# Five added matmuls on zeros at the start of a planned attention and feed-forward kernel, and another table of planner rules

## The chip, the cores and the metric

The kernel runs on one core of a Trainium2 chip. The metric is the time of one execution on the device in microseconds (us). Four compute engines and the DMA queues work side by side and meet only at semaphores: TensorE (PE, matmuls; PEld in the profile is its weight load), VectorE (DVE), ScalarE (ACT) and GpSimd (POOL). SyncE (SP) issues most of the transfers. The profile also has the clock that TensorE was granted, as a share of its full clock.

## The reference

```python
mod = (_silu(c) @ w_mod).reshape(c.shape[0], 6, 1, -1)
sa, ca, ga, sb, cb, gb = (mod[:, i] for i in range(6))         # six rows of 512
h = _layernorm(x) * (1 + ca) + sa
x = x + ga * _A_ref(h, A_wqkv, A_wo)                           # attention, 32 heads of 16
h = _layernorm(x) * (1 + cb) + sb
x = x + gb * ((_gelu(h @ w_gate) * (h @ w_up)) @ w_down)       # 512 -> 1792 -> 512
```

x has 2048 tokens of 512 numbers in bf16. Attention is full: every one of 32 heads has 2048 x 2048 scores, softmax(q k / 4), and then a product with v.

## The kernel before

**Tiling.** Queries are worked on in sets of columns (SETS: seven of 256, two of 128; the first two go together as 512 for the first four groups of heads). For one set and one group of four heads (a "unit"), keys come in tiles of 128. A *slot* is one bank of PSUM, 128 keys by 512 columns of scores. There are 2048 slots, and their order is fixed when the program is written. Scores go to ps_sc, which is two halves of three banks. A *chunk* of two or three slots fills one half (`qk`, recorded at L361 like every matmul), and then one ACT instruction exponentiates it into the tile E (L374). PE multiplies E with the values (`pv_mms`, into ps_pv or the last bank of ps_sc).

**Two engines for the exponential.** ACT does most slots. For some groups of four slots, called *quads*, DVE does it by writing the scaled score as the bits of a bf16 number (uint16, L386, out of ps_sc into kq, dreg, mreg or onorm) and by making three shifted copies of the four slots (128x2048 uint16, L386). PE adds the four versions up with correspondingly scaled values (tile vs). One slot of a quad goes into a chunk beside two slots for ACT.

**Planner.** The kernel is written by a planner that runs when the program is built (`stream`). It keeps a model of each engine's free time, and at each step it records the next instruction in each engine's queue: a chunk of scores, a round of values, a *side* step (projections, feed-forward of finished sets, on ps_mi), a filler matmul, or a DVE task (`step`, `background`). Engines then run their queues in that order, and only semaphores hold them. The planner puts in filler matmuls (`filler`) when the matmul columns that it has logged in the last 3413 ns are under FILL = 3700. The added matmuls are logged too.

**Rules.** The planner's choices follow a tuple of 14 numbers, `self.tune`. The table TUNE has 33 of them, and `rules` takes the row of the current stage, that is of the slot position divided by STEP = 64. The rules, numbered from 0: 0 how far ACT must be ahead before other work goes in front of scores; 1 the credit of side work under which a quad may be opened late; 2 the backlog of DVE tasks at which no quad is opened; 3 how far ahead DVE tasks may go before a quad's slot; 4 and 5 how late DVE may be (after the present, after ACT) when it takes a slot; 6 and 7 when a quad's shifted copies become urgent, by the rounds left in its unit; 8 and 9 how near and how far a quad's slots may lie; 10 and 11 the credit that lets a side step go in front; 12 the rate of that credit in per cent; 13 how far ahead DVE's background tasks are placed.

**The start.** `prologue` loads the first tokens, warms PE up on a tile of zeros (`warm`, 17 matmuls of 128x512 into ps_mi), computes the modulation columns, layer norms, transposes and projects the first 512 tokens for four head groups. At its end ACT and DVE evict queries and keys (qT, kT). Then `stream` takes over; after chunk 0 it calls `prologue_rest` (keys of the second 256 tokens, then the masks of `split_q` on DVE, which clear odd or even heads in the queries), and after chunk 2 `prologue_v`. From `stream` on, `mm` splits a whole matmul into four of 32 output columns (`self.split`).

## Time and profile before

| | us |
|---|---|
| median of three runs (lowest, highest) | 813.16 (811.11, 813.68) |
| the profiled execution | 813.47 |
| its span, first to last instruction | 811.7 |
| busy: ACT, PE, DVE, POOL | 777.2, 751.3, 749.9, 4.9 |
| first exponential of scores, end of the last one | 13.2, 783.8 |
| mean granted TensorE clock | 0.992 |

A line of a group reads: line of the program, engine, operation, tile written, tiles read, shapes and count, then busy time and mean duration of one, then the idle time of the engine just before and what ended it. A line of the timeline has start and duration in us first. A group that merges several instructions has the time from the first start to the last end. A line of the view by stretches has start and end, length, busy time of each engine with its count of instructions, granted clock, share of the DMA engines, and GB/s.

### The profile page before, as it was taken

To read this page: it belongs to the slowest core of one execution; us is meant where nothing else is said; L and a number is where in the kernel's file an instruction comes from. 1 tells how busy PE (TensorE), PEld (TensorE's weight loads), DVE (VectorE), ACT (ScalarE), POOL (GpSimd) and SP (SyncE) were. 2 spreads that over 40 slices of the span, in tenths; PEclk is the share of its full clock that TensorE was granted. 3 is DMA by queue.
4 is the path that set the end of the run, shared out by engine and by line. 5 is a ranking of instruction groups with operands and counts; after the bars stand their busy time and mean duration, and the time that the engine had idled before them with its cause. 6 is when DMAs were issued, how large, how long until landed. Compare 5 with 4: busy or idle time off the path is not lost.

```text
span 811.7 us, 37453 instructions
## 1 busy us (share of the span) xinstructions
PE 751.3 (93%) x17217; PEld 367.2 (45%) x17217; DVE 749.9 (92%) x1512; ACT 777.2 (96%) x746; POOL 4.9 (1%) x13
## 2 busy tenths in 40 slices
PE   7989899998989998998999999999898999998998
PEld 3333334343444454444534444345443543355666
DVE  6776899999999999999999999999999999999963
ACT  5899999999999999999999999999999999999962
POOL 2000000000000000000000000000000000000000
PEclk8799999999999999999999999999999999999999
DMA  9100000012562044104420442025333532300000
GB/s 301 58 2 17 15 10 11 11 28 60 151 206 55 17 139 130 52 16 126 131 69 17 125 122 66 23 61 153 88 75 100 167 96 63 94 10 12 18 12 15
DMA packets 96404, 59.23 MB, mean 73 GB/s; under 512 B 17141, under 2 KB 93814, under 8 KB 96246
## 3 DMA queue, kind: packets, MB, share of 16 engines
q1 hardware_dynamic: 95716, 56.30, 24.7%
q8 instruction: 135, 2.21, 1.1%
q10 hardware_dynamic: 530, 0.53, 0.2%
q14 instruction: 23, 0.19, 0.1%
HBM read 50.04 MB, written 4.18 MB: 67 GB/s over the span
## 4 chain that ended last, share of the span: by engine, by line
ACT 72%; PE 14%; DVE 11%; DMA 2%; issue 1%; SPq 0%; DVEq 0%
ACT E L374 70%; PE ps_sc L361 6%; PE ps_mi L361 5%; PE ps_pv L361 3%; ACT wreg L374 2%; DVE dreg L386 2%; DVE mreg L386 2%; DVE wreg L395 1%; DVE wreg L378 1%; DVE kq L386 1%; DMA mreg<-in_B_w_up_dram 1%; DVE wreg L391 1%; DMA mreg<-in_B_w_gate_dram 1%; DVE wreg L386 0%; DMA xs<-in_A_x_dram 0%
## 5 line engine op out<-in xcount | busy, mean ns | idle before, releaser
L374 ACT ACTIVATE E<-ps_sc 128x1024 bf16<-128x1024 f32 (+2 forms) x700 | 751.6, 1306 | 20.5 <-PE ps_sc L361 20.2
L361 PE MATMUL ps_sc<-qT,kT 32*128 32x256 bf16 (+3 forms) x2048 | 200.0, 274 | 20.9 <-ACT E L374 17.5
L361 PE MATMUL ps_sc<-qo,kT 32*128 32x256 bf16 (+2 forms) x2048 | 197.7, 274 | 17.1 <-ACT E L374 14.7
L361 PE MATMUL ps_pv<-E,vaug 128*17 128x256 bf16 (+2 forms) x3168 | 152.8, 274 | 0.7 <-DVE vaug L395 0.3
L386 DVE TENSOR_SCALAR dreg<-ps_sc 128x512 uint16<-128x512 f32 x208 | 140.3, 683 | 6.4 <-PE ps_sc L361 5.5
L361 PE MATMUL ps_mi<-wreg,mreg 128*32 128x256 bf16 x2816 | 112.0, 275 | 6.5 <-DVE wreg L391 2.2
L361 PEld LDWEIGHTS ps_sc<-qT,kT 32*128 32x128 bf16 (+1 forms) x2048 | 60.4, 92 | 110.4 <-ACT E L374 93.0
L361 PEld LDWEIGHTS ps_sc<-qo,kT 32*128 32x128 bf16 x2048 | 60.2, 92 | 108.5 <-ACT E L374 94.7
L361 PEld LDWEIGHTS ps_pv<-E,vaug 128*17 128x17 bf16 x3168 | 60.2, 89 | 58.0 <-issue 38.7
L361 PEld LDWEIGHTS ps_mi<-wreg,mreg 128*32 128x32 bf16 x2816 | 64.9, 96 | 39.6 <-issue 22.6
L386 DVE TENSOR_SCALAR kq<-ps_sc 128x512 uint16<-128x512 f32 x108 | 72.8, 682 | 5.1 <-PE ps_sc L361 5.0
L386 DVE TENSOR_SCALAR mreg<-ps_sc 128x512 uint16<-128x512 f32 x100 | 67.2, 683 | 2.4 <-PE ps_sc L361 2.1
L361 PE MATMUL ps_pv<-mreg,vs 128*17 128x256 bf16 (+2 forms) x1552 | 67.0, 267 | 2.5 <-issue 1.4
L386 DVE TENSOR_SCALAR mreg<-dreg 128x2048 uint16<-128x2048 uint16 x93 | 62.2, 678 | 0.0
L361 PEld LDWEIGHTS ps_pv<-mreg,vs 128*17 128x17 bf16 x1552 | 33.7, 91 | 14.9 <-issue 5.4
L361 PE MATMUL ps_mi<-hreg,wreg 128*32 128x512 bf16 (+1 forms) x496 | 37.8, 381 | 0.7 <-DVE qT L386 0.6
L395 DVE CAST wreg<-ps_mi 128x512 bf16<-128x512 f32 x49 | 33.4, 681 | 1.0 <-PE ps_mi L361 0.6
L378 DVE TENSOR_TENSOR wreg<-wreg 128x1024 bf16<-128x1024 bf16 (+1 forms) x56 | 34.2, 611 | 0.0
L391 DVE SCALAR_TENSOR_TENSOR wreg<-wreg,ps_mi 128x512 bf16<-128x512 bf16 x49 | 33.2, 678 | 0.9 <-PE ps_mi L361 0.7
L386 DVE TENSOR_SCALAR mreg<-mreg 128x2048 uint16<-128x2048 uint16 x49 | 32.7, 681 | 0.0
L395 DVE COPY osb<-ps_pv 128x256 f32<-128x256 f32 (+2 forms) x63 | 25.9, 411 | 4.9 <-PE ps_pv L361 4.6
L374 ACT ACTIVATE wreg<-wreg 128x1024 bf16<-128x1024 bf16 (+1 forms) x28 | 30.2, 1080 | 0.0
(203 smaller groups left out, 777.6 us busy)
## 6 DMA issues: line engine op xcount, KB each, us to landing
mreg<-in_B_w_up_dram SPq DMA_DIRECT2D x46, 256.0 KB, 3.1
mreg<-in_B_w_gate_dram SPq DMA_DIRECT2D x42, 256.0 KB, 3.2
rb<-scr_rec SPq DMA_DIRECT2D x120, 32.0 KB, 1.9
dreg<-wd_scaled SPq DMA_DIRECT2D x15, 256.0 KB, 3.9
mreg<-wd_scaled SPq DMA_DIRECT2D x10, 256.0 KB, 4.3
ereg<-wd_scaled SPq DMA_DIRECT2D x10, 256.0 KB, 3.8
mreg<-in_w_mod_dram SPq DMA_DIRECT2D x1, 2048.0 KB, 12.4
out_dram<-xs SPq DMA_DIRECT2D x15, 128.0 KB, 1.8
```

The source lines that it names most:

```text
L361: return self.rec("pe", lambda e: e.matmul(out, lhsT, rhs, start=start, stop=stop, tile_position=tp), [lhsT, rhs], [out], cost=(n, int(rhs ...
L374: return self.rec("act", lambda e: e.activation(out, in_, func, scale=scale, **kw), rd, wr, cost=self.cost("act", out, [in_], "act"))
L378: return self.rec(eng, lambda e: e.tensor_tensor(out, a, b, op), [a, b], [out], cost=self.cost(eng, out, [a, b], "tt"))
L386: return self.rec(eng, lambda e: e.tensor_scalar(out, a, s1, s2, **kw), rd, [out], cost=self.cost(eng, out, [a], "ts") + 60 * (len(rd) - 1 ...
L391: return self.rec("dve", lambda e: e.scalar_tensor_tensor(out, a, s, b, op0=op0, op1=op1), rd, [out], cost=self.cost("dve", out, [a, b], " ...
L395: return self.rec(eng, lambda e: e.tensor_copy(out, in_), [in_], [out], cost=self.cost(eng, out, [in_], "ts"))
```

## The change

Two calls are added: one matmul on the tile of zeros behind the last projection of the prologue, and four behind the key projection in `prologue_rest`. Each writes ps_mi, which nobody reads in that state. The one in the prologue is a single 128x128 by 128x512 instruction; the four others are split into four instructions each. And each of the 33 rows of TUNE gets other numbers. No function is changed otherwise. Rows 0 to 10 and 28 to 32 of the old and of the new table, and the two calls:

```diff
 TUNE = (
-    (1000, 4097, 6, 120, 700, 150, 2, 9, 96, 30, 2, 1536, 100, 150),
-    (600, 3500, 6, 120, 700, 150, 2, 3, 96, 30, 2, 1536, 100, 150),
-    (600, 3500, 6, 120, 700, 150, 2, 3, 96, 27, 3, 1536, 100, 0),
-    (600, 3500, 6, 120, 700, 150, 2, 3, 64, 27, 3, 3500, 100, 400),
-    (600, 3500, 5, 120, 700, 150, 2, 3, 96, 30, 2, 3500, 125, 150),
-    (1000, 2500, 5, 120, 700, 450, 2, 3, 96, 30, 2, 3500, 125, 100),
-    (600, 3500, 6, 120, 700, 150, 2, 9, 96, 30, 2, 1536, 100, 150),
-    (600, 3500, 6, 120, 500, 150, 2, 9, 96, 30, 2, 1536, 100, 400),
-    (600, 3500, 6, 120, 700, 150, 4, 9, 96, 30, 2, 1536, 100, 250),
-    (600, 3500, 6, 120, 700, 150, 2, 9, 96, 30, 2, 1536, 110, 150),
-    (600, 3500, 7, 120, 500, 450, 2, 9, 96, 30, 2, 1536, 110, 150),
...
-    (600, 4097, 6, 120, 500, 150, 2, 16, 128, 24, 2, 1536, 125, 400),
-    (600, 4097, 6, 120, 500, 150, 2, 9, 48, 30, 2, 1536, 125, 400),
-    (600, 3500, 6, 120, 500, 0, 2, 16, 96, 34, 2, 1536, 100, 400),
-    (600, 2500, 6, 120, 1100, 150, 2, 9, 96, 30, 0, 1536, 80, 150),
-    (600, 2500, 6, 120, 1100, 150, 2, 9, 96, 30, 0, 1536, 80, 150),
+    (800, 3500, 6, 120, 700, 0, 0, 9, 48, 30, 3, 800, 100, 150),
+    (600, 3500, 6, 60, 700, 450, 2, 16, 96, 30, 2, 1536, 100, 250),
+    (600, 3000, 6, 60, 700, 450, 2, 16, 64, 30, 2, 1536, 100, 400),
+    (600, 3500, 6, 0, 1100, 150, 2, 9, 96, 30, 2, 3500, 110, 400),
+    (600, 3500, 6, 0, 1100, 150, 2, 9, 96, 30, 2, 800, 110, 400),
+    (600, 3500, 6, 0, 1100, 150, 1, 16, 96, 30, 3, 3500, 100, 400),
+    (600, 3500, 5, 120, 500, 450, 2, 3, 96, 34, 2, 2500, 100, 400),
+    (600, 3500, 5, 120, 500, 450, 2, 3, 96, 34, 2, 2500, 100, 400),
+    (1000, 3500, 5, 120, 500, 450, 2, 3, 96, 30, 2, 2500, 125, 400),
+    (1000, 3500, 5, 120, 900, 450, 2, 3, 96, 30, 2, 3500, 125, 400),
+    (600, 4097, 5, 120, 900, 450, 2, 3, 96, 24, 2, 1536, 90, 400),
...
+    (600, 3500, 5, 0, 700, 150, 2, 9, 128, 38, 2, 1536, 80, 150),
+    (450, 3500, 3, 120, 700, 150, 2, 9, 96, 30, 2, 1536, 100, 0),
+    (300, 3500, 6, 0, 700, 150, 2, 6, 128, 24, 2, 1536, 110, 150),
+    (800, 3500, 6, 120, 900, 0, 2, 16, 96, 30, 2, 1536, 100, 150),
+    (800, 3500, 6, 120, 900, 0, 2, 16, 96, 30, 2, 1536, 100, 150),
 )
@@
             for n, dc in enumerate((3, 0, 1, 2) if h == 0 else (2, 0, 3, 1)):
                 for out, col in ((qb[h], 0), (kb, 512))[:2 - h]:
                     self.mm(out, self.wqkv[:, dc, col:col + P], self.hT[:, dc, hs], start=(n == 0), stop=(n == NDC - 1))
+        self.warm_up(1)
         for h in range(2):
             self.act(self.qT[:, 0, 256 * h:256 * h + 256], qb[h], ACT.Copy, scale=Q_SCALE)
         self.copy(dve, self.kT[:, 0, 0:256], kb)
@@
         for dc in range(NDC):
             self.mm(self.pv[:, 256:512], self.wqkv[:, dc, 512:512 + P], self.hT[:, dc, 256:512], start=(dc == 0), stop=(dc == NDC - 1))
+        self.warm_up(4)
         self.copy("dve", self.kT[:, 0, 256:512], self.pv[:, 256:512])
```

## The prediction

> **What bounds the kernel now.** I read the page's slices first, then busy time by stretch, the groups of ScalarE (ACT) and VectorE (DVE), and last the timeline of the first 29 us.

> ```profile
> ACT  5899999999999999999999999999999999999962
> PEclk8799999999999999999999999999999999999999
> 28.80:85.00 56.20, 51.49 (x949) 20.01 (x945) 41.62 (x110) 55.97 (x52) 0.56 (x1) 1.00 0.04 9
> 110.00:745.00 635.00, 592.13 (x13986) 285.24 (x13986) 619.10 (x1174) 634.25 (x603) 0.00 (x0) 1.00 0.29 79
> 783.80:811.70 27.90, 23.36 (x348) 19.60 (x336) 11.87 (x34) 7.05 (x14) 0.00 (x0) 1.00 0.04 11
> ```

> The columns of the last three lines are the stretch, its length, then busy time of PE, PEld, DVE, ACT and POOL, the granted clock, and DMA. From 28.8 to 745 us ACT is never idle to speak of (55.97 of 56.20, 634.25 of 635.00). So the time there is what ACT has to do, and only the hand-over of score slots to DVE makes it less. The last 27.9 us, after the final exponential, are a serial tail. What is left is the start, where PEclk shows an 8 and a 7. The same view cut at the clock's edges:

> ```profile
> 8.13:11.54 3.41, 2.76 (x41) 2.14 (x41) 3.06 (x13) 2.29 (x4) 0.00 (x0) 1.00 1.14 312
> 11.54:14.95 3.41, 1.66 (x29) 0.86 (x28) 1.76 (x6) 2.22 (x3) 0.00 (x0) 1.00 1.10 339
> 14.95:18.37 3.42, 3.26 (x71) 1.75 (x70) 2.04 (x6) 2.49 (x3) 0.00 (x0) 0.50 1.08 357
> 21.78:25.19 3.41, 3.41 (x24) 1.10 (x20) 1.49 (x7) 2.21 (x3) 0.00 (x0) 0.50 0.44 155
> 25.19:28.60 3.41, 3.41 (x36) 0.95 (x33) 2.64 (x14) 2.77 (x3) 0.00 (x0) 0.50 0.02 5
> 28.60:32.02 3.42, 3.23 (x46) 1.37 (x43) 2.92 (x9) 3.21 (x3) 0.00 (x0) 1.00 0.00 0
> ```

> PE was busy for only 1.66 of the 3.41 us before 14.95, and there the clock halves, for 13.65 us. During this time PE is full (3.41 of 3.41), and ACT waits for it. These are ACT's exponentials of that stretch, each with the idle time before it:

> ```profile
> 13.17 1.45 ACT L374 ACTIVATE E<-ps_sc 128x1536 bf16<-128x1536 f32 x1 [0.58 <-PE ps_sc L361]
> 15.46 2.37 ACT L374 ACTIVATE E<-ps_sc 128x1024 bf16<-128x1024 f32 x2 [0.84 <-PE ps_sc L361]
> 18.25 1.02 ACT L374 ACTIVATE E<-ps_sc 128x1024 bf16<-128x1024 f32 x1 [0.42 <-PE ps_sc L361]
> 19.67 2.36 ACT L374 ACTIVATE E<-ps_sc 128x1536 bf16<-128x1536 f32 x2 [0.40 <-PE ps_sc L361]
> 23.23 3.71 ACT L374 ACTIVATE E<-ps_sc 128x1536 bf16<-128x1536 f32 x3 [1.20 <-PE ps_sc L361]
> 27.33 1.02 ACT L374 ACTIVATE E<-ps_sc 128x1024 bf16<-128x1024 f32 x1 [0.39 <-PE ps_sc L361]
> 28.81 1.45 ACT L374 ACTIVATE E<-ps_sc 128x1536 bf16<-128x1536 f32 x1 [0.46 <-PE ps_sc L361]
> ```

> The six waits after the first exponential add up to 0.84 + 0.42 + 0.40 + 1.20 + 0.39 + 0.46 = 3.71 us. ACT runs without a gap afterwards, so what is won here moves everything behind it forward.

> **The change, part by part.** *The five matmuls.* They stand in two holes of PE:

> ```profile
> 11.57 0.60 PE L361 MATMUL ps_sc<-hreg,wreg 128*128 128x256 bf16 x4
> 12.73 0.39 PE L361 MATMUL ps_sc<-qT,kT 16*128 16x512 bf16 x3 [0.56 <-ACT qT L374]
> 13.06 0.62 PE L361 MATMUL ps_pv<-hreg,wreg 128*32 128x256 bf16 x16
> 14.45 0.35 DVE L386 TENSOR_SCALAR qT<-qT,rm 128x512 bf16<-128x512 bf16 x1
> 14.86 0.98 PE L361 MATMUL ps_sc<-qT,kT 16*128 16x512 bf16 x5 [1.19 <-DVE qT L386]
> 20.63 1.47 PE L361 MATMUL ps_mi<-xs,ident 128*32 128x512 bf16 x12
> 28.69 0.40 PE L361 MATMUL ps_mi<-xs,ident 128*32 128x512 bf16 x4
> 7.87 0.38 PE L361 MATMUL ps_mi<-dreg 128*128 128x512 bf16 x1
> ```

> The one of the prologue is a whole 128x512 matmul, 0.38 us to its end, in a hole of 0.56 us: nothing. The four of prologue_rest are split into four instructions each, 16 in all, with as many weight loads. One set takes 0.40 us at full clock; three at half clock took 1.47 us, 0.43 us apart after a first 0.60, so about 0.21 us apart at full clock. Four sets: 3 x 0.21 + 0.40 = 1.04 us, in a hole of 1.19 us. What hides them is DVE, which masks the queries until 14.80 us; the scores behind them on PE need that. Without this cover they would cost their 1.04 us. The evictions wait for earlier matmuls, not for these. The bank that they write, ps_mi, was last read by ACT before 11.54:

> ```profile
> 10.53 1.01 ACT L374 ACTIVATE hreg<-ps_mi,modA 128x256 bf16<-128x256 bf16 x2
> ```

> They add 0.38 + 1.04 us to 1.66, so about 3.1 of 3.41 us busy, more than the 2.76 of the window before, after which the clock stayed whole. I take it that the clock then stays at 1.00.

> Worth: PE's scores come at full speed. Of the first wait (0.84 us) DVE's mask sets most; the scores end 0.2 us sooner (0.39 instead of about 0.6). The other five waits, 2.87 us, stand in a stretch in which PE is the full engine and its work halves; I take them as gone. Gain 0.2 + 2.87 = 3.1 us. Bounds: 3.7 us (all of it) and -0.5 us (the clock halves while they run: four sets at 0.43 are 1.7 us in a hole of 1.19). I take 3.1 because DVE, next in line, is busy for only 1.49 and 2.64 us of the two later windows. Late next is DVE's chain of layer norms, which itself waits for PE there.

> [...]

> *The table.* It changes the order of the work, not its amount, except for the number of quads (four score slots that DVE computes with shifted copies instead of ACT).

> ```profile
> L374 ACT ACTIVATE E<-ps_sc 128x1024 bf16<-128x1024 f32 x448 | 449.5, 1164 | 2.7 <-PE ps_sc L361 2.4
> L374 ACT ACTIVATE E<-ps_sc 128x1536 bf16<-128x1536 f32 x244 | 363.6, 1591 | 4.5 <-PE ps_sc L361 4.5
> L386 DVE TENSOR_SCALAR dreg<-ps_sc 128x512 uint16<-128x512 f32 x208 | 140.3, 683 | 6.4 <-PE ps_sc L361 5.5
> L386 DVE TENSOR_SCALAR kq<-ps_sc 128x512 uint16<-128x512 f32 x108 | 72.8, 682 | 5.1 <-PE ps_sc L361 5.0
> L386 DVE TENSOR_SCALAR mreg<-ps_sc 128x512 uint16<-128x512 f32 x100 | 67.2, 683 | 2.4 <-PE ps_sc L361 2.1
> L386 DVE TENSOR_SCALAR mreg<-dreg 128x2048 uint16<-128x2048 uint16 x93 | 62.2, 678 | 0.0
> ```

> A chunk of three slots keeps ACT for 363.6/244 = 1.490 us, one of two for 449.5/448 = 1.003. A quad takes a slot from each of four chunks: 4 x 0.487 = 1.95 us less on ACT, for 4 x 0.683 + 3 x 0.68 = 4.77 us more on DVE. How many quads the new table gives, no view of this kernel shows. Bounds: DVE idles 56.20 - 41.62 = 14.6 us between 28.8 and 85, room for three more at most, a gain of 5.9 us; three fewer cost as much. I take none, since new rows loosen some rules and tighten others (below). The tail's order may shift by about 1 us either way: the table's last rows touch it, but its 27.9 us are a chain.

> Sum for the profiled execution (813.47 us, its span 811.7 and 1.8 around it): 813.5 - 3.1 = 810.4. It lies 0.3 above the median of the three runs, 813.16; against that median I predict **810.1 us**.

> **The rivals.** *More quads early (806.2).* Rows 1 and 2 raise rule 7 from 3 to 16, which puts the shifted copies ahead of DVE's other tasks and so frees their buffers sooner. For it:

> ```profile
> 56.98 0.69 DVE L386 TENSOR_SCALAR kq<-ps_sc 128x512 uint16<-128x512 f32 x1 [1.14 <-PE ps_sc L361]
> 60.39 0.63 DVE L386 TENSOR_SCALAR sq<-kq 128x2048 uint16<-128x2048 uint16 x1
> 64.57 0.68 DVE L386 TENSOR_SCALAR onorm<-kq 128x2048 uint16<-128x2048 uint16 x1
> 72.35 0.69 DVE L395 CAST vaug<-ps_mi 128x512 bf16<-128x512 f32 x1 [1.71 <-PE ps_mi L361]
> ```

> A quad's last slot is done at 57.7, its last copy only at 65.2. Against it: behind 70 us DVE waits for value projections, which no rule of these rows brings sooner. Two more quads give 810.1 - 3.9 = 806.2.

> *The clock is lost anyway (813.2 to 813.7).* The matmuls do not hold it, because what counts is not PE's busy time: from 21.8 to 25.2 us PE was full and the clock stayed at 0.50, or because a later window falls short. Against: the whole-array zeros are denser work than the tiles of those windows. Time: as before, or up to 0.5 us more. [...]

> *Fewer quads in the middle (816), slower.* Rule 2, the DVE backlog at which no quad is opened, goes from 6, 6, 6, 6, 7 to 5 in rows 6 to 10, and from 6, 6 to 5, 3 in rows 28 and 29. A row holds for 64 of 2048 slots, (783.8 - 13.2)/32 = 24 us; seven rows are 168 us. In the long stretch there are 95 quads:

> ```profile
> L386 DVE TENSOR_SCALAR dreg<-ps_sc 128x512 uint16<-128x512 f32 x192 | 129.5, 683 | 5.7 <-PE ps_sc L361 5.0
> L386 DVE TENSOR_SCALAR kq<-ps_sc 128x512 uint16<-128x512 f32 x96 | 64.6, 682 | 1.4 <-PE ps_sc L361 1.3
> L386 DVE TENSOR_SCALAR mreg<-ps_sc 128x512 uint16<-128x512 f32 x92 | 61.9, 683 | 1.9 <-PE ps_sc L361 1.6
> ```

> (192 + 96 + 92)/4 = 95 in 635 us, so 25 in those rows. ACT has no slack to hide a lost one. It decides from three lost of 25: 3 x 1.95 = 5.9 us against a gain of 3.1 is 2.7 us slower than before, 810.1 + 5.9 = 816.0. Against it: rows 6 to 9 also let DVE run 450 instead of 150 ns behind ACT, which admits more, and a quad refused for backlog can often be opened a chunk later.

> **How the numbers follow.** A measurement of this kernel tells about 0.3% (2.4 us) from no change. Chances: clock held and quads about as many 0.50 (own range 807.5 to 812); more quads 0.13; clock lost 0.15; fewer quads 0.22. Below 810.7 lie the second and four fifths of the first: 0.53. Above 815.6 lie the last and a little of the clock case joined with a lost quad: 0.25. Within: 0.22. The range runs from 805.5 (between two and three quads more) to 816.5 (three fewer and a little).

> **What would show it.** The granted clock at 1.00 from 14.95 to 28.6 us, ACT's waits for scores before 29 us near 0.6 instead of 3.7, the scores after the mask not later than 14.9 us: the first part is right. The count of DVE's 128x512 uint16 writes from ps_sc in the three groups above, now 208 + 108 + 100 = 416, over four gives the quads: 104 means that my zero is right, 101 or fewer the slower rival, 106 the faster. A clock of 0.50 after the added matmuls, or ACT waiting for scores between 29 and 745 us, would make the prediction wrong.

## The result, and the profile after

| | us |
|---|---|
| median of the changed kernel, 22 runs (lowest, highest) | 811.02 (808.65, 816.78) |
| median of the kernel before on the same chip, 22 runs | 815.00 (811.11, 820.90) |
| ratio, with its 95% interval | 0.996 (0.9941 to 0.998) |
| the profiled execution, its span | 808.65, 806.9 (before 813.47, 811.7) |

The change makes the kernel 0.4% faster (0.2 to 0.6%). The profiled executions differ by 4.8 us. The slices of ACT and of the clock of the changed kernel:

```profile
ACT  6999999999999999999999999999999999999972
PEclk9999999999999999999999999999999999999999
```

The clock no longer dips: its mean is 1.000, where it was 0.992. Busy time by stretch of 3.41 us, from the one with the second hole on (columns as before: stretch, length, PE, PEld, DVE, ACT, POOL, clock, DMA):

```profile
12.95:16.37 3.42, 3.10 (x103) 1.75 (x98) 2.65 (x8) 2.75 (x3) 0.00 (x0) 1.00 1.10 331
16.37:19.78 3.41, 2.68 (x31) 0.84 (x29) 3.13 (x13) 3.41 (x4) 0.00 (x0) 1.00 1.05 394
19.78:23.19 3.41, 2.65 (x40) 1.14 (x38) 2.84 (x12) 3.41 (x4) 0.00 (x0) 1.00 1.02 381
```

ACT, which was busy for 2.2 to 3.0 us of such a stretch, has the 0.67 us wait in the first of these three and fills the other two. ACT's timeline of the first 30 us shows one wait behind the first chunk where there were six:

```profile
12.95 1.45 ACT L374 ACTIVATE E<-ps_sc 128x1536 bf16<-128x1536 f32 x1 [0.58 <-PE ps_sc L361]
15.07 15.93 ACT L374 ACTIVATE E<-ps_sc 128x1024 bf16<-128x1024 f32 x14 [0.67 <-PE ps_sc L361]
```

In the timeline of PE and DVE there, the four added sets (16 instructions) lie under DVE's mask:

```profile
12.84 0.62 PE L361 MATMUL ps_pv<-hreg,wreg 128*32 128x256 bf16 x16
13.29 1.04 PE L361 MATMUL ps_mi<-dreg 128*32 128x512 bf16 x16
14.23 0.35 DVE L386 TENSOR_SCALAR qT<-qT,rm 128x512 bf16<-128x512 bf16 x1
14.64 0.60 PE L361 MATMUL ps_sc<-qT,kT 16*128 16x512 bf16 x5 [0.32 <-DVE qT L386]
```

They take the 1.04 us of the sum, and the scores start when the mask ends, with 0.32 us of PE to spare. (The record of the single matmul in the first hole is missing from this trace; its weight load at 11.68 us is there.)

What is left of the 4.8 us is seen in ACT's waits for scores: total, times, longest. The kernel before, in the stretches 14 to 31, 31 to 700 and 700 to 784 us (the first includes the 0.58 us ahead of the first chunk):

```profile
ACT E L374 <- PE ps_sc L361: 4.3, 7, 1.2
ACT E L374 <- PE ps_sc L361: 0.2, 1, 0.2
ACT E L374 <- PE ps_sc L361: 2.3, 4, 1.3
```

The changed kernel, in the same stretches:

```profile
ACT E L374 <- PE ps_sc L361: 1.2, 2, 0.7
ACT E L374 <- PE ps_sc L361: 1.2, 4, 0.5
ACT E L374 <- PE ps_sc L361: 0.7, 2, 0.5
```

4.3 to 1.2 at the start is 3.1 us less (3.71 - 0.67 = 3.04 in the finer rows); 1.0 more in the middle; 1.6 less at the end. The rest of the 4.8 is a first chunk 0.2 us earlier, 0.8 less ACT work between the first and the last chunk (764.1 to 763.3 us without the waits), and a tail shorter by 0.3 us. The number of quads is the same, (208 + 108 + 100)/4 = 104; these are the changed kernel's groups:

```profile
L386 DVE TENSOR_SCALAR dreg<-ps_sc 128x512 uint16<-128x512 f32 x208 | 140.0, 684 | 7.1 <-PE ps_sc L361 6.0
L386 DVE TENSOR_SCALAR kq<-ps_sc 128x512 uint16<-128x512 f32 x108 | 73.3, 684 | 3.7 <-PE ps_sc L361 3.2
L386 DVE TENSOR_SCALAR mreg<-ps_sc 128x512 uint16<-128x512 f32 x100 | 67.1, 682 | 1.0 <-PE ps_sc L361 0.7
```

### The profile page after: what moved, and what is told of

It reads as the page before. It is cut to its first block, busy times and chain, and to the rows that moved or that the text cites. A ratio compares the mean times of both kernels' runs of the same rounds, so it can differ in the third digit from the quotient of the medians.

```text
span 806.9 us, 37455 instructions
## 1 busy us (share of the span) xinstructions
PE 748.4 (93%) x17214; PEld 366.9 (45%) x17218; DVE 749.4 (93%) x1512; ACT 776.5 (96%) x746; POOL 4.6 (1%) x13
## 3 DMA queue, kind: packets, MB, share of 16 engines
q8 instruction: 135, 2.21, 1.1%
## 4 chain that ended last, share of the span: by engine, by line
ACT 80%; PE 11%; DVE 6%; DMA 2%; issue 1%; SPq 0%; DVEq 0%
ACT E L374 77%; PE ps_sc L361 5%; PE ps_mi L361 4%; PE ps_pv L361 2%; ACT wreg L374 2%; DVE dreg L386 1%; DVE mreg L386 1%; DVE wreg L395 1%; DMA scr_rec<-rden 1%; DMA xs<-in_A_x_dram 0%; DMA dreg<-in_B_w_down_dram 0%; DMA rb<-scr_rec 0%; DMA mreg<-in_B_w_up_dram 0%; DVE dreg L378 0%; DVE st L414 0%
## 5 line engine op out<-in xcount | busy, mean ns | idle before, releaser
L374 ACT ACTIVATE E<-ps_sc 128x1024 bf16<-128x1024 f32 (+2 forms) x700 | 751.1, 1312 | 16.6 <-PE ps_sc L361 16.3
L361 PE MATMUL ps_sc<-qT,kT 32*128 32x256 bf16 (+3 forms) x2048 | 197.0, 273 | 20.8 <-ACT E L374 18.6
L361 PE MATMUL ps_sc<-qo,kT 32*128 32x256 bf16 (+2 forms) x2048 | 194.6, 273 | 18.5 <-ACT E L374 15.9
L361 PE MATMUL ps_pv<-E,vaug 128*17 128x256 bf16 (+2 forms) x3172 | 152.5, 272 | 1.7 <-DVE osb L395 0.8
L386 DVE TENSOR_SCALAR dreg<-ps_sc 128x512 uint16<-128x512 f32 x208 | 140.0, 684 | 7.1 <-PE ps_sc L361 6.0
L361 PE MATMUL ps_mi<-wreg,mreg 128*32 128x256 bf16 x2816 | 114.9, 275 | 3.9 <-DVE wreg L395 2.2
L361 PEld LDWEIGHTS ps_sc<-qo,kT 32*128 32x128 bf16 x2048 | 59.8, 92 | 111.2 <-ACT E L374 101.0
L361 PEld LDWEIGHTS ps_sc<-qT,kT 32*128 32x128 bf16 (+1 forms) x2048 | 59.7, 92 | 107.4 <-ACT E L374 94.9
L361 PEld LDWEIGHTS ps_pv<-E,vaug 128*17 128x17 bf16 x3172 | 60.3, 89 | 58.8 <-issue 39.8
L361 PEld LDWEIGHTS ps_mi<-wreg,mreg 128*32 128x32 bf16 x2816 | 64.0, 96 | 39.6 <-issue 23.8
L386 DVE TENSOR_SCALAR kq<-ps_sc 128x512 uint16<-128x512 f32 x108 | 73.3, 684 | 3.7 <-PE ps_sc L361 3.2
L361 PE MATMUL ps_pv<-mreg,vs 128*17 128x256 bf16 (+2 forms) x1528 | 68.8, 268 | 0.1
L386 DVE TENSOR_SCALAR mreg<-ps_sc 128x512 uint16<-128x512 f32 x100 | 67.1, 682 | 1.0 <-PE ps_sc L361 0.7
L386 DVE TENSOR_SCALAR mreg<-dreg 128x2048 uint16<-128x2048 uint16 x93 | 62.6, 680 | 0.0
L361 PEld LDWEIGHTS ps_pv<-mreg,vs 128*17 128x17 bf16 x1528 | 33.3, 90 | 11.8 <-issue 5.1
L361 PE MATMUL ps_mi<-hreg,wreg 128*32 128x512 bf16 (+1 forms) x496 | 37.2, 376 | 0.1
L395 DVE CAST wreg<-ps_mi 128x512 bf16<-128x512 f32 x49 | 33.4, 682 | 1.4 <-PE ps_mi L361 1.2
L386 DVE TENSOR_SCALAR mreg<-mreg 128x2048 uint16<-128x2048 uint16 x49 | 33.2, 680 | 0.0
L374 ACT ACTIVATE wreg<-wreg 128x1024 bf16<-128x1024 bf16 (+1 forms) x28 | 30.4, 1085 | 0.2 <-DVE wreg L378 0.2
L395 DVE COPY osb<-ps_pv 128x256 f32<-128x256 f32 (+2 forms) x63 | 25.9, 411 | 3.2 <-PE ps_pv L361 3.1
```

The lines of the kernel that those rows point to most:

```text
L361: return self.rec("pe", lambda e: e.matmul(out, lhsT, rhs, start=start, stop=stop, tile_position=tp), [lhsT, rhs], [out], cost=(n, int(rhs ...
L374: return self.rec("act", lambda e: e.activation(out, in_, func, scale=scale, **kw), rd, wr, cost=self.cost("act", out, [in_], "act"))
L386: return self.rec(eng, lambda e: e.tensor_scalar(out, a, s1, s2, **kw), rd, [out], cost=self.cost(eng, out, [a], "ts") + 60 * (len(rd) - 1 ...
L395: return self.rec(eng, lambda e: e.tensor_copy(out, in_), [in_], [out], cost=self.cost(eng, out, [in_], "ts"))
```

## The experiments

All ratios are against the kernel before, run on the same chip in the same job. Runs of one kernel differ by several us, for reasons shown in part below, so a profile's waits and the medians are read together. The two profiles above come from quick runs: 808.65 us is the fastest of the 22 runs of the changed kernel, and 813.47 is under the median of the kernel before.

| run | median us (runs) | before | ratio (95%) |
|---|---|---|---|
| five matmuls alone | 812.79 (10) | 816.14 | 0.9949 (0.9930 to 0.9967) |
| table alone | 812.00 (7) | 816.14 | 0.9938 (0.9909 to 0.9967) |
| five thin matmuls | 815.12 (12) | 816.14 | 0.9987 (0.9968 to 1.0006) |
| the change | 810.70 (6) | 816.14 | 0.9929 (0.9906 to 0.9953) |
| last rows new, in the old order | 813.61 (12) | 816.34 | 0.9975 (0.9952 to 0.9997) |
| last rows old, in the new order | 812.82 (12) | 816.34 | 0.9952 (0.9930 to 0.9973) |
| one matmul | 816.68 (10) | 816.34 | 1.0001 (0.9977 to 1.0025) |
| nine matmuls | 814.24 (10) | 816.34 | 0.9976 (0.9956 to 0.9996) |
| the change, holes filled | 811.95 (12) | 813.59 | 0.9975 (0.9957 to 0.9993) |
| the change, third time | 809.52 (12) | 813.59 | 0.9946 (0.9923 to 0.9969) |
| old order, five matmuls, holes filled | 815.50 (12) | 813.59 | 1.0016 (0.9997 to 1.0035) |
| five matmuls alone, again | 812.04 (12) | 813.59 | 0.9983 (0.9961 to 1.0005) |

### Which half of the change gains: matmuls alone, table alone, both

The matmuls are put into the old order behind the planner's back, so that every queue but PE's stays as it was:

```diff
+    def unplanned(self, f):
+        kept = dict(self.free), self.pe_issue, self.pe_end, self.pe_mode, list(self.tile_free), len(self.log)
+        f()
+        self.free, self.pe_issue, self.pe_end, self.pe_mode, self.tile_free, n = kept
+        del self.log[n:]
...
+        self.unplanned(lambda: self.warm_up(1))
...
+        self.unplanned(lambda: self.warm_up(4))
```

> The order of the kernel before, instruction for instruction, with the five matmuls put in and nothing else (the planner does not see them). My theory, that the matmuls hold the clock: granted clock 1.00 throughout, ACT's waits for scores before 29 us fall from 3.7 to about 0.7, time 3.0 to 3.3 us (0.4%) below the kernel before. The rival, that the new order makes the gain: the clock may hold, but less than 1 us is gained, since the old order was written without them.

The other way round, the changed kernel's planner counts the matmuls and they are not issued:

```diff
+    def ghost_up(self, n):
+        for _ in range(n):
+            for j in range(4) if self.split else (None,):
+                self.model(_Op("pe", "pe", 0, None), self.free["pe"], (512, P, None if j is None else (0, 32 * j)))
...
-        self.warm_up(1)
+        self.ghost_up(1)
...
-        self.warm_up(4)
+        self.ghost_up(4)
```

> The order of the changed kernel, instruction for instruction, without the five matmuls (the planner still counts them, so that nothing else moves). My theory: the clock halves near 15 us for some 10 to 14 us, ACT waits 3 us or more for scores there, and the time is 1 to 2 us below the kernel before (what the shorter waits behind 745 us are worth). The rival, that the new order makes the gain: 4 us or more below the kernel before, as the changed kernel.

> The changed kernel itself, on the same chip as the other three, for comparison: 4 to 5 us below the kernel before in the profile; granted clock 1.00 throughout.

Each half gains, and they overlap. ACT's waits in the same three stretches, matmuls alone:

```profile
ACT E L374 <- PE ps_sc L361: 1.3, 2, 0.7
ACT E L374 <- PE ps_sc L361: 0.2, 1, 0.2
ACT E L374 <- PE ps_sc L361: 3.0, 5, 1.3
```

and table alone:

```profile
ACT E L374 <- PE ps_sc L361: 2.9, 5, 0.9
ACT E L374 <- PE ps_sc L361: 2.8, 8, 0.6
ACT E L374 <- PE ps_sc L361: 1.1, 2, 0.8
```

The matmuls do what the theory says, in the start alone: 3.0 us off the waits, 3.35 off the median. The new order takes nothing there that depends on them; behind 700 us it has about two us less of waits than the run with the matmuls alone (3.0 against 0.7, and 0.3 and 1.3 in the two later traces of the change). Without the matmuls its clock halves too, at 15.33 us, but only for 6.8 us instead of 13.65, so that there the matmuls are worth 2.9 - 1.2 = 1.7 us of waits. On this chip the medians are 816.14 before, 812.79 with the matmuls, 810.70 with the table as well; that is 3.35 and then 2.1 us. In the later job the two steps were 1.55 and 2.5 us, and there the matmuls alone are not told from no change (0.9961 to 1.0005). So the size of each step is known to a us or two, no better. My expectation for the table alone, 1 to 2 us, was too low: the medians differ by 4.1 us, the interval of the ratio is 2.7 to 7.4 us. The clock was lost there for a shorter time than I had reckoned. The profiles do not account for the rest. Over all three stretches the table alone waits 6.8 us, as much as the kernel before; the matmuls alone 4.5 us (a trace of the quickest of its ten runs), and the three traces of the change 3.1, 4.7 and 5.5 us. What the new order saves behind 700 us it loses in part between 31 and 700 us (1.2, 3.1 and 2.9 us of waits against 0.2). That the table is worth about 2 us rests on the medians, which agree in direction in both jobs.

### What holds the clock: busy time, or how much of the array works

Five matmuls of the same length at the same places, each on a sixteenth of the array:

```diff
+    def thin_up(self, n, m):
+        for _ in range(n):
+            self.mm(self.mi[0:32, :], self.warm[0:32, 0:32], self.warm[0:32, :], tp=(0, 0))
...
+        self.unplanned(lambda: self.thin_up(1, 1))
...
+        self.unplanned(lambda: self.thin_up(4, 1))
```

> The order of the kernel before, with five matmuls of 512 columns put in at the two places, but each on one corner of 32 rows by 32 columns of the array (a sixteenth), so that PE is busy at the same places. If the clock goes by the share of time in which PE is busy, it holds at 1.00 and the time is as in the run with whole matmuls (3 us below before). If it goes by how much of the array works, which I take for likelier, the clock halves near 15 us as before, and the time is within 0.5 us of the kernel before.

Busy time of the run with thin matmuls, in the window before the clock falls and in the next:

```profile
12.33:15.74 3.41, 2.94 (x57) 1.23 (x60) 1.96 (x6) 2.16 (x3) 0.00 (x0) 1.00 1.10 336
15.74:19.15 3.41, 3.16 (x65) 1.38 (x53) 2.51 (x11) 3.03 (x4) 0.00 (x0) 0.50 1.07 379
```

PE is busy for 2.94 of 3.41 us and the clock halves; in the changed kernel it held after windows with 2.65 and 2.68. So busy time does not sort these windows. (The four in the second hole are one instruction each here, so they also have fewer weight loads; the count that follows does not rest on this run alone.)

The windows are read from the clock itself. In the kernel before it was 1.00 from 4.71 to 14.95 us, 0.50 from there to 28.60 us and 1.00 to the end of the span; the spells of 10.24 and 13.65 us are three and four times 3.41. It was 0.50 for 6.83 us at the start of the run with thin matmuls and of that with the table alone, and for 3.41 us in the second trace of the changed kernel (635.61 to 639.02 us): two and one times. All the spells at half clock in the fourteen traces, up to the last exponential of scores, were one, two or four times 3.41 us long.

I counted every matmul of a window as its columns times the share of 128 x 128, in steps of 32, that its shape fills (a whole 128x512 matmul is 512, a set of four on 32 output columns also 512, scores of three row groups 384). At full clock one whole 128x512 followed the other every 0.216 us (from 805.79 us of the kernel before), so 3.41 us have room for about 8090 such columns. In the same traces, up to the same point, the full clock fell after eighteen windows, which had 2168 to 3076 columns by this count, and was kept after all others, over 3100 windows; the lowest of these had 2943. What these traces show is that overlap, from 2943 to 3076, and not a line within it. The few matmuls in f32 are counted here by their columns, once or twice. They last longer than that: the two instructions of one product on 128 columns, from 787.41 us of the kernel before, took 0.28 us, as long as five times 128 columns at 0.216 us per 512. Counted four times, one of the eighteen (at 759.65 us in the run with one matmul) would have 3524. The share of the array sorts these windows better than the columns alone: counted by the used quarters of the output columns alone, with all rows taken as used, the clock fell after windows with up to 7316 and was kept from 3321 up. Before the change the window from 11.54 us had 2701; with the added 5 x 512 that sum is over 5000, and the clock stayed at 1.00.

The other dose, one matmul alone, tests the count from below:

```diff
+        self.unplanned(lambda: self.warm_up(1))
```

> The order of the kernel before with only the first added matmul, the whole one in the hole of 0.56 us. Counted as columns times the share of the array that works, the window before the clock halves held 2701, and no window under about 3000 kept the clock; 512 more make 3200, just over. My theory, that this sum must stay over about 3000 in every window of 3.41 us wherever the grid of windows lies: one matmul helps in some positions of the grid and not in others, and more often than not the clock still halves near 15 us; gain 0 to 2 us. Rival, that any work in the hole is enough: clock 1.00 before 29 us, gain 3 us.

The ACT timeline of that run begins

```profile
14.98 3.28 ACT L374 ACTIVATE E<-ps_sc 128x1024 bf16<-128x1024 f32 x3 [0.67 <-PE ps_sc L361]
18.59 2.37 ACT L374 ACTIVATE E<-ps_sc 128x1536 bf16<-128x1536 f32 x2 [0.33 <-PE ps_sc L361]
22.15 2.37 ACT L374 ACTIVATE E<-ps_sc 128x1536 bf16<-128x1536 f32 x2 [1.20 <-PE ps_sc L361]
```

and its clock halved at 15.55 us behind a window with 3076 columns, in which PE was busy for 1.94 us: this much work in the hole was not enough, and no gain is measured (1.0001).

### The price without cover

Eight sets instead of four in the second hole, in the old order:

```diff
+        self.unplanned(lambda: self.warm_up(1))
...
+        self.unplanned(lambda: self.warm_up(8))
```

> The order of the kernel before with one matmul in the first hole and eight instead of four in the second, which is 1.19 us long. Eight sets take 7 x 0.21 + 0.40 = 1.9 us, so by my sum the scores behind them end 0.6 to 0.9 us later than in the run with five, ACT's second chunk starts as much later, and the time is that much above the run with five. Rival: the extra sets are hidden as well, and nothing changes against five.

The timeline around the hole:

```profile
13.62 1.90 PE L361 MATMUL ps_mi<-dreg 128*32 128x512 bf16 x32
15.45 0.60 PE L361 MATMUL ps_sc<-qT,kT 16*128 16x512 bf16 x5
15.88 2.37 ACT L374 ACTIVATE E<-ps_sc 128x1024 bf16<-128x1024 f32 x2 [1.15 <-PE ps_sc L361]
```

Eight sets last 1.90 us, as summed, and now PE has no idle time before the scores. ACT waits 1.15 instead of 0.67 us: the four extra sets cost 0.48, a little less than expected. The medians (814.24, and 812.79 in another job with five) cannot settle half a microsecond.

### Where the table's part comes from

Rows 28 to 32 hold from slot 1792 on. First the old order with only these rows new (and the five unplanned matmuls), then the changed kernel with only these rows old:

```diff
-    (600, 4097, 6, 120, 500, 150, 2, 16, 128, 24, 2, 1536, 125, 400),
-    (600, 4097, 6, 120, 500, 150, 2, 9, 48, 30, 2, 1536, 125, 400),
-    (600, 3500, 6, 120, 500, 0, 2, 16, 96, 34, 2, 1536, 100, 400),
-    (600, 2500, 6, 120, 1100, 150, 2, 9, 96, 30, 0, 1536, 80, 150),
-    (600, 2500, 6, 120, 1100, 150, 2, 9, 96, 30, 0, 1536, 80, 150),
+    (600, 3500, 5, 0, 700, 150, 2, 9, 128, 38, 2, 1536, 80, 150),
+    (450, 3500, 3, 120, 700, 150, 2, 9, 96, 30, 2, 1536, 100, 0),
+    (300, 3500, 6, 0, 700, 150, 2, 6, 128, 24, 2, 1536, 110, 150),
+    (800, 3500, 6, 120, 900, 0, 2, 16, 96, 30, 2, 1536, 100, 150),
+    (800, 3500, 6, 120, 900, 0, 2, 16, 96, 30, 2, 1536, 100, 150),
```

> The order of the kernel before with the five matmuls put in (as in the run with the matmuls alone), but rows 28 to 32 of the new table from slot 1792 on (about 700 us); rows 0 to 27 stay old. What is to be explained: the two runs with the new order wait 0.8 and 1.2 us for scores between 700 us and the last chunk, the three with the old order 2.5 to 3.4. Theory: the new last rows make the difference, and here the waits behind 700 us are about 1 us, and the time is 1.5 to 2 us below the run with the matmuls alone (809 to 811). Rival: the state that the earlier rows leave makes it; then the waits stay at 2.5 us or more and the time is as in that run or worse.

```diff
-    (600, 3500, 5, 0, 700, 150, 2, 9, 128, 38, 2, 1536, 80, 150),
...
-    (800, 3500, 6, 120, 900, 0, 2, 16, 96, 30, 2, 1536, 100, 150),
+    (600, 4097, 6, 120, 500, 150, 2, 16, 128, 24, 2, 1536, 125, 400),
...
+    (600, 2500, 6, 120, 1100, 150, 2, 9, 96, 30, 0, 1536, 80, 150),
```

> The changed kernel with rows 28 to 32 of the old table; all before slot 1792 is the changed kernel's order. Theory (the last rows make the difference): waits for scores behind 700 us go up to 2.5 us or more, time 1.5 to 2 us above the changed kernel. Rival (the state left by the earlier rows makes it): waits stay near 1 us and the time is the changed kernel's.

ACT's waits from 700 to 784 us, last rows new in the old order:

```profile
ACT E L374 <- PE ps_sc L361: 4.4, 3, 2.7
```

and last rows old in the new order:

```profile
ACT E L374 <- PE ps_sc L361: 1.8, 2, 1.4
```

The new last rows alone do not bring the short waits: with the earlier rows old, the total of 4.4 us lies in the upper part of the 2.3 to 4.9 of the seven traces with the old table throughout, and the time is not better than with the matmuls alone. Taken out of the new order, they leave 1.8 us, between those and the 0.3 to 1.3 of the three traces of the change. But in both runs one wait makes most of the total, 2.71 and 1.43 us, each behind a stop of PE inside a series of value matmuls (2.55 us from 752.85, 1.72 us from 751.06) for which the profile shows no cause. So the totals do not decide between my theory and its rival.

A single wait of the old order says more. It stands ahead of the last four chunks of three slots; in the kernel before:

```profile
776.26 0.62 PE L361 MATMUL ps_pv<-mreg,vs 128*17 128x128 bf16 x32
776.71 1.03 PE L361 MATMUL ps_mi<-xs,hreg 128*32 128x512 bf16 x16
777.57 0.40 PE L361 MATMUL ps_pv<-E,vaug 128*17 128x128 bf16 x16
777.90 0.40 PE L361 MATMUL ps_sc<-qo,kT 32*128 32x128 bf16 x12
778.34 5.48 ACT L374 ACTIVATE E<-ps_sc 128x1536 bf16<-128x1536 f32 x4 [1.27 <-PE ps_sc L361]
```

PE is busy, but with values and feed-forward that the planner put ahead of the scores. All seven traces with the old table have this wait (1.27 us in six, 1.68 in one). None of the seven others has it, and among these are both runs here: the new last rows remove it behind the old earlier rows, and the new earlier rows remove it ahead of the old last ones. So 1.3 us of what the table saves behind 700 us are this one place, and it takes old rows in both parts of the table to make it. The rest is open, and the medians (0.9952 against 0.9929 and 0.9946 for the whole table) do not separate the run with the last rows old from the change.

### Why one kernel's runs differ, and a try at more

In the second trace of the changed kernel the clock was lost elsewhere:

```profile
632.19:635.61 3.42, 2.08 (x49) 0.79 (x49) 3.42 (x7) 3.42 (x5) 0.00 (x0) 1.00 0.76 241
635.61:639.02 3.41, 3.41 (x53) 1.56 (x44) 1.85 (x4) 3.08 (x4) 0.00 (x0) 0.50 0.25 73
```

The same order in the first trace has as little work there, 2719 columns where this window has 2712. But its window, from 630.8 us, begins 0.85 us earlier with respect to that work, has 3214 columns, and kept the clock. So I take it that where the windows lie decides which thin places fall into one of them, and that differs by execution: the first fall came at 14.95, 15.33, 15.55 and 15.74 us in the four traces of the kernel before, the table alone, one matmul and thin matmuls. Over the 40 runs of the changed kernel the time follows the run's mean granted clock (correlation -0.92): 0.85 us for each us of clock lost, from about 809 at full clock, where one window at half clock counts as 1.7 us lost. If so, filling the thin places should help. Zero weights times anything were added to open sums, wherever the planner saw PE idle, behind its back:

```diff
+                    self.mm(acc_of(u)[32 * j:32 * j + VW, 0:w], self.zero[:, 0:VW], filler[1][:, 0:w], start=False, stop=False, tp=(0, 32 * j))
```

> The changed kernel's order with 196 more sets of matmuls by zero weights, added to sums that are open in PE's planned idle moments between about 22 and 755 us; the planner does not see them, and the other engines' queues stay the same. What is to be explained: the changed kernel runs between 808.7 and 816.8 us, and the time falls as the granted clock rises. Theory: single windows of 3.41 us in which the array works too little halve the clock for a window, at other places in each execution since the grid of windows lies elsewhere; filled, the clock stays near 1.00 in all runs, the median falls by 1 to 2 us against the changed kernel on the same chip, to 808.5 to 809.5, and the spread shrinks. Rival: the extra matmuls stand in the way of scores (196 sets of 0.1 to 0.2 us); ACT's waits between 31 us and the last chunk rise by 2 us or more and the time with them.

> The changed kernel itself beside the other three, for comparison on the same chip: 810 to 812 us.

> The old order with the five matmuls, and with matmuls by zero weights put into its planned idle moments in the same way. If the clock is all that parts the old order from the new one, it comes to the time of the filled new order within 1 us. If the table is worth about 2 us of waits behind 700 us, as the profiles say, it stays 2 us above that one.

> The old order with the five matmuls again, for comparison on the same chip. Of its first ten runs four had a clock of 1.000, two of them at 809.5 and two at 812.5 and 813.2 us, so something else than the clock moves it by 3 us; if this profile falls on a slow one, ACT's waits will show where. Time 811 to 814 us; waits before 29 us 0.7 us.

Of the first theory half is right. With the fill the mean clock goes from 0.9978 to 0.9989, and 8 of 12 runs keep it to the end, against 5 of 12. The time gets worse all the same: 811.95 against 809.52 in the new order, 815.50 against 812.04 in the old. The profile that was taken does not show the price; ACT's waits in the three stretches are no longer than in the unfilled run beside it (1.3, 2.6, 0.5 against 1.3, 2.9, 1.3):

```profile
ACT E L374 <- PE ps_sc L361: 1.3, 2, 0.7
ACT E L374 <- PE ps_sc L361: 2.6, 5, 1.1
ACT E L374 <- PE ps_sc L361: 0.5, 1, 0.5
```

But that profile is one of the quicker runs (810.25 us; the eight runs at full clock spread from 808.2 to 813.3). So where the extra matmuls cost the time is not shown, and the clock is not all that moves it. Filled, the old order is 3.5 us slower than the new one, so the gain of the table isn't only a matter of the clock. No version faster than the change came out of this. The last run, the matmuls alone once more, was a slower one (816.49 us) whose clock was lost for four windows, with 4.8 us of waits in the middle.

What parts quick and slow runs at full clock is seen in part in two traces of the changed kernel that both kept it. PE and ACT in the quickest run (808.65 us):

```profile
233.27 0.52 PE L361 MATMUL ps_mi<-wreg,mreg 128*32 128x256 bf16 x8 [1.02 <-DVE wreg L395]
234.16 4.34 ACT L374 ACTIVATE E<-ps_sc 128x1536 bf16<-128x1536 f32 x4 [0.26 <-PE ps_sc L361]
```

and in the third trace (811.22 us):

```profile
234.62 0.40 PE L361 MATMUL ps_mi<-wreg,mreg 128*32 128x256 bf16 x8 [2.12 <-DVE wreg L395]
235.39 4.34 ACT L374 ACTIVATE E<-ps_sc 128x1536 bf16<-128x1536 f32 x4 [1.24 <-PE ps_sc L361]
320.07 0.40 PE L361 MATMUL ps_mi<-wreg,mreg 128*32 128x256 bf16 x8 [1.04 <-DMA mreg<-in_B_w_up_dram]
320.83 1.94 ACT L374 ACTIVATE E<-ps_sc 128x1024 bf16<-128x1024 f32 x2 [0.75 <-PE ps_sc L361]
```

Matmuls of the feed-forward stand ahead of scores in PE's queue and wait for a transfer: at 320 us for weights, and at 233 us for DVE's work behind the softmax denominators (rb<-scr_rec), which landed at 231.80 us in one trace and 233.15 in the other. ACT waits (1.24 - 0.26) + 0.75 = 1.7 us longer for it, of the 2.6 us between the two runs. Such a wait also thins out a window: in that last, slower run PE stands still for 1.50 us from 322.44 us, waiting for the same weights; the first half of that lies in the window from 319.80, which has 2549 columns, and the clock halves behind it. So late transfers lose time with and without the clock, and part of the 0.85 us may be theirs.

## Why the prediction was right

I forecast 810.1 us, 0.38% less; measured are 811.02, 0.4% less than the kernel before on the same chip. The cause that I named, the clock held at the start, is shown. That the number came so close is in part luck: 810.1 was counted from a median of three runs, 813.16, where 22 runs give 815.00, and the medians fell by 4.0 us instead of 3.1, since the table was worth something that I had put at nothing.

*The five matmuls, 3.1 us.* Right in place, cause and size: clock at 1.00, 3.04 us off the waits, 1.04 us for the four sets, hidden behind the mask, which the nine-matmul run bears out (0.48 us once the cover is gone). By medians the matmuls alone gained 3.35 us in one job and 1.55 in another. Right for a wrong reason in one step: I argued from PE's busy time (3.1 of 3.41 us, more than the window before). The thin matmuls fill the same time (PE busy for 2.94 of 3.41 us) and the clock fell to 0.50 all the same; what sorted the windows in these traces is the share of the array that works. My remark in the rival, that whole-array zeros are denser work, was the argument that the runs bear out.

*Idle or thin.* In no trace here was PE idle for a window before its last microseconds: the clock fell after windows with PE busy for 1.41 to 2.97 us of 3.41 (1.66 in the kernel before, 2.94 with the thin matmuls).

*The table, 0.* This term was too small. The quads stayed at 104, as I took it, so both rivals that counted quads were wrong in their mechanism. But I priced the order only by quads and the tail, and not by the waits for scores before the last chunk, 2.3 us in the kernel before, which I had in the trace and left out of the sum. The new order has 1.6 us less of them in the profile, 1.27 of it in one place, and the medians of the change lie 2.1 and 2.5 us under the matmuls alone. How the rest of that comes about is not shown.

*The tail.* 0.3 us, inside the 1 us that I gave it.

*The clock-lost rival.* It did not happen at the start in any of the ten traces with all five whole matmuls or more. Its second condition, a later window that falls short, did come true in some of them, as single windows from 87 us on; I had priced it as the loss of the whole gain, and it is a part of the 8 us over which the runs spread. One of my own signs of being wrong, waits of ACT between 29 and 745 us, came true too in small: 1.2 to 3.1 us of them between 31 and 700 us in the three traces of the change.

## What to carry to other kernels

Where the granted clock dips, look at the 3.41 us before the dip and count columns times the share of the array used: here the clock fell after 2168 to 3076 of them. A hole of PE in which another engine sets the path could be filled with matmuls on zeros for nothing, as long as they ended before the next real matmul might start: four sets of 1.04 us fitted into 1.19 us, eight cost 0.48 us. Fill a hole whose cover is known, and not all the holes that a plan shows: filling them all raised the mean clock from 0.9978 to 0.9989 and lost 2.4 us here. When an order changes, price the waits ahead of the bounding engine over the whole span, not only the amount of work, and look at what stands in front of its input in the queue that feeds it.
